# Two groups of loads put off, a row of norms written from another queue, and three additions moved in an attention and gated-FFN kernel

## The chip, the cores and the metric

The kernel runs on one core of a Trainium2 chip. The metric is the device time of one execution in microseconds (us); the number quoted is the median of several executions.

## The reference

Four batches, each with 6016 rows and 256 channels. Attention runs over channels, so its score matrix is 256 x 256 per batch; the result, 24064 rows of 256, goes through a gated feed-forward layer with 1536 hidden units.

```python
qn = q / (norm(q, axis=1) + 1e-6)          # q, k, v: (4, 6016, 256)
kn = k / (norm(k, axis=1) + 1e-6)
s = kn.transpose(0, 2, 1) @ qn / tau       # (4, 256, 256), tau = 1
a = exp(s - s.max(-1)); a /= a.sum(-1) + 1e-9
x = (v @ a).reshape(24064, 256)
out = (sigmoid(x @ w_gate) * (x @ w_val)) @ w_out
```

## The kernel before, in words

**Folding.** The softmax matrix of a batch is small, so the kernel multiplies it into the two weight matrices first: G = a @ w_gate and H = a @ w_val (tiles `gh_G`, `gh_H`, 16 pieces a batch in batch 0, 12 later). Then only v has to be streamed: gate = v @ G, val = v @ H, hidden = sigmoid(gate) * val, out = hidden @ w_out.

**Tiling.** A batch has 47 row tiles of 128 rows, in 12 chunks of four (three in the last). A chunk runs over 12 slots f, one per 128 hidden units. `glu(b, ci, f)` (L495) does a slot: two 512-column matmuls into `ps_gate`, two into `ps_val` (two PSUM banks each, so a slot's matmuls need the banks of two slots ago to be read out), a tanh on ACT into `g_sb` (L516), and on DVE `hT` = (g_sb + 1) * ps_val (L517). The output product of a chunk is done one chunk later, in pieces spread over the next chunk's slots (`run_work`), as a Strassen-like scheme with seven products; its sums of hidden tiles are made by DVE (`sums`, L539, in slots 7 to 11 of the chunk itself and 1 and 3 to 6 of the next). ACT copies a finished `ps_o` to `m_sb` (L593) or `out_sb` (L600), and POOL (GpSimd) makes the last additions (L594, L595, L610, L611). Batch 0's chunk 0 has a plain product and no sums.

**Order of the work.** It is written out by hand: instructions stay on each engine in the order in which the Python emits them. `side_work(b)` (L749) builds a table of side jobs for a batch; `at(slot, fn, ...)` puts one behind slot `slot` (chunk * 12 + f) of batch b. Such jobs are, for the batch after: loading q and k by groups of four tiles (`load_qk`, L138, issued by POOL, cast to bf16 on the way), the score matmuls (`score`, into `ps_s`), squares on ACT (`acc_square`, L248) and their running sums on DVE (`acc_add`, L286), and at the end the norms and the softmax. In batch 0 the groups start at slots s0 = 14, 20, 27, 34, 41, 48, 55, 61, 68, 75, 82, 89, and the additions stand at s0 + 3 and s0 + 7 (none for the first group). Loads of v (`load_v`, L148) are issued by POOL two chunks ahead, at f = 0; a chunk of v is transposed by a DMA from SP (`transpose_v`, L481) one chunk ahead, at f = 2. SP also issues the output stores (L652). All these queues work through their instructions in order, so an instruction that waits holds up those behind it.

**Start.** Batch 0 has no batch before it: its scores run alone, to about 33 us. Then come its softmax and the first four pieces of G and H. Pieces 4 to 15 are put between the slots of chunk 0: `gh_mid` (L813) names the piece that goes between the gate and the val matmuls of slot f, `gh_end` (L814) those behind it. POOL meanwhile loads v, the weights and w_out, in float32, casts w_out (`copy_w_out`, L212, slot 8) and makes sums of its blocks (`w_sums`, L217, from slot 10).

**Norms.** Behind slot 108 of a batch (chunk 9, f = 0) `norms_inv` (L361, L362) makes the inverse norms of the next batch, one value a channel. Those of k have to lie along a row on all partitions: `spread_both` (L313) transposes them on DVE into `rT` (L317), writes a row of 256 values to DRAM with two DMAs (L320) and reads it back to all 128 partitions (L324, `rk_sb`), all on SP's queue. `scale_x` (L304, `x_sb`) uses it on DVE behind slots 120 and 122.

Of the kernel before, what the change touches and what calls it, by code (L numbers as in the profile page):

```python
# [9 lines left out]
FP32 = mybir.dt.float32  # L10
# [43 lines left out]
def kernel(  # L54
# [20 lines left out]
    nc = tc.nc  # L75
# [5 lines left out]
    B, N, C = q.shape  # L81
# [4 lines left out]
    FC = DFF // P  # L86
# [15 lines left out]
    def pool(name, bufs, **kw):  # L102
        return ctx.enter_context(tc.tile_pool(name=name, bufs=bufs, **kw))
# [14 lines left out]
    dpool = pool("dpool", 1, space=bass.MemoryType.DRAM)  # L118
# [8 lines left out]
    def mm(out, lhsT, rhs, start, stop, **kw):  # L127
        nc.tensor.matmul(out, lhsT=lhsT, rhs=rhs, start=start, stop=stop, **kw)  # L128
# [23 lines left out]
    t0, nt = groups0[0]  # L152
# [72 lines left out]
    st = {}  # L225
# [87 lines left out]
    def spread_both(b):  # L313

        s = st[b]
        rT = attp.tile([P, 32], FP32, tag="rT", name="rT")
        nc.vector.transpose(out=rT, in_=r_wide)  # L317
        row = dpool.tile([C], FP32, tag="row", name="row")
        for i in range(CB):
            nc.sync.dma_start(  # L320
                out=row[ds(i * P, P)].rearrange("(s j) -> s j", j=32), in_=rT[CB + i : P : 32, :]
            )
        s["rk_sb"] = attp.tile([P, C], FP32, tag="rk", name="rk_sb")
        nc.sync.dma_start(out=s["rk_sb"], in_=row.rearrange("(o c) -> o c", o=1).to_broadcast([P, C]))  # L324

# [115 lines left out]
    gh_first = [(f0, nf, w, i) for f0, nf in pieces for w in range(2) for i in range(CB)]  # L441

    def gh_mms(b, piece, pl, tag):
        s = st[b]
        f0, nf, w, i = piece
        ps = pl.tile([P, FG], FP32, tag=tag, name="ps_gh")
        for j in range(CB):
            mm(
                ps[:, :nf],
                s["e"][i][:, j, :],  # L450
                w_sb[w][f0 // FG][:, j, ds(f0 % FG, nf)],
                start=(j == 0),
                stop=(j == CB - 1),
            )
        return ps

    def gh_store(b, piece, ps, act):
        s = st[b]
        f0, nf, w, i = piece
        dst = s["gh"][w][f0 // FG][:, i, ds(f0 % FG, nf)]  # L460
        if act:
            nc.scalar.activation(out=dst, in_=ps[:, :nf], func=ACT.Copy, scale=s["rrow"][i][w])
        else:
            nc.vector.tensor_scalar(  # L464
                out=dst, in0=ps[:, :nf], scalar1=s["rrow"][i][w], scalar2=None, op0=ALU.mult
            )

    def gh(b, piece, pl, tag, act=None):
        gh_store(b, piece, gh_mms(b, piece, pl, tag), piece[3] == 0 if act is None else act)
# [25 lines left out]
    def glu(b, ci, f, between=None):  # L495
        t0, nt = groups[ci]
        n = nt * P
        G, H = st[b]["gh"]
        vT = vts[b, ci]
        if f == 0:  # L500
            hts[b, ci] = hpool.tile([P, FC, CH], BF16, tag="hT", name="hT")
        ps_gate = psg.tile([P, CH], FP32, tag="g", name="ps_gate")
        ps_val = psv.tile([P, CH], FP32, tag="v", name="ps_val")
        for ps, w in ((ps_gate, G), (ps_val, H)):
            for ib in range(CB):
                mm(
                    ps[:, :n],
                    w[f // (FG // P)][:, ib, ds(f % (FG // P) * P, P)],
                    vT[:, ib, :nt, :],
                    start=(ib == 0),  # L510
                    stop=(ib == CB - 1),
                )
            if between is not None and w is G:
                between()
        g_sb = gpool.tile([P, CH], FP32, tag="g", name="g_sb")
        nc.scalar.activation(out=g_sb[:, :n], in_=ps_gate[:, :n], func=ACT.Tanh, scale=0.5)  # L516
        nc.vector.scalar_tensor_tensor(  # L517
            out=hts[b, ci][:, f, :n],
            in0=g_sb[:, :n],
            scalar=1.0,  # L520
            in1=ps_val[:, :n],
            op0=ALU.add,
            op1=ALU.mult,
        )
# [171 lines left out]
    for g, (t0, nt) in enumerate(groups0):  # L696
# [6 lines left out]
        while adds:  # L703
            w, last_sq = adds.pop()
# [44 lines left out]
    def side_work(b):  # L749


        side = {}

        def at(slot, fn, *a):
            side.setdefault(divmod(slot, FC), []).append((fn, a))

        for ci in range(NCH):
            nb, nci = (b, ci + 1) if ci + 1 < NCH else (b + 1, 0)
            lb, lci = (b, ci + 2) if ci + 2 < NCH else (b + 1, ci + 2 - NCH)
            if nb < B:  # L760
                at(ci * FC + 2, transpose_v, nb, nci)
            if lb < B:
                at(ci * FC + 0, load_v, lb, lci)
            if (b, ci) == (0, 0):
                for i in range(FC // TPC):
                    at(8, copy_w_out, i)
                for n, m in enumerate((1, 0, 3, 2, 4)):
                    for i in range(FC // TPC):
                        at(10 + 2 * n, sum_w_out, m, i)
        n = b + 1  # L770
        if n == B:
            return side
        first, last = (14 if b == 0 else 0), 8 * FC
        for g, (t0, nt) in enumerate(groups):
            s0 = first + g * (last - first) // NCH
            if b == 0:
                at(max(0, s0 - 12), load_qk, n, t0, nt)
            elif s0 >= 24:
                at(s0 - 24, load_qk, n, t0, nt)
            for u in range(nt):  # L780
                at(first + (t0 + u) * (last - first) // NT, score, n, t0, u)
            if g == 0:
                at(s0, acc_start, n)
            for i, (fn, w) in enumerate(((acc_square, 0), (acc_add, 0), (acc_square, 1), (acc_add, 1))):
                at(s0 + 1 + 2 * i, fn, n, g, w)
        if n + 1 < B:
            for g, (t0, nt) in enumerate(groups[:3]):
                at(NCH * FC - 24 + 8 * g, load_qk, n + 1, t0, nt)
        s0 = 8 * FC + 2
        at(s0 if b == 0 else s0 - 2, acc_fold, n, 0)  # L790
        at(s0 + 1 if b == 0 else s0, acc_fold, n, 1)
        at(s0 + 3, norms_mm, n)
        at(s0 + 4, root_seed, n)
        at(s0 + 4, root_steps, n)
        at(s0 + 10, norms_inv, n)
        at(s0 + 10, spread_both, n)
        at(s0 + 22, scale_x, n, 0)
        at(s0 + 24, scale_x, n, 1)
        at(s0 + 25, exps, n, 0)
        at(s0 + 26, exps, n, 1)  # L800
        at(s0 + 28, all_sums, n)
        at(s0 + 28, gh_tiles, n)
        for i, piece in enumerate(gh_order):
            slot = s0 + 29 + 2 * i
            if slot < NCH * FC:
                at(slot, gh, n, piece, *((pss, "s"), (psm, "m"))[i % 2])
            else:
                spill.setdefault((n, *divmod(slot - NCH * FC, FC)), []).append((gh, (n, piece, psm, "m")))
        return side

    gh_mid = {0: 4, 1: 6, 2: 9, 3: 11}  # L813
    gh_end = {0: (5,), 1: (7, 8), 2: (10,), 3: (12,), 4: (13,), 5: (14,), 6: (15,)}  # L814
    gh_banks = ((pso, "o"), (psm, "m"), (pso, "o"), (pss, "s"))

    def gh_piece(n):
        gh(0, gh_first[n], *gh_banks[n % 4])

    prev = None  # L820
    for b in range(B):
        side = side_work(b)
        for ci in range(NCH):
            final = (b, ci) == (B - 1, NCH - 1)
            for f in range(FC):
                mid = gh_mid.get(f) if (b, ci) == (0, 0) else None
                glu(b, ci, f, None if mid is None else (lambda: gh_piece(mid)))
                if prev is not None:
                    if f == 4:
                        store()  # L830
                    if f + final in NEXT_SLOTS and prev != (0, 0):
                        a_sum(*prev, 1, NEXT_SLOTS[f + final])
                    run_work(work, 1 / max(1, FC - final - f))
                if f in OWN_SLOTS and not final and (b, ci) != (0, 0):
                    a_sum(b, ci, 0, OWN_SLOTS[f])
                for fn, a in spill.get((b, ci, f), []) + side.get((ci, f), []):
                    fn(*a)
                if (b, ci) == (0, 0):
                    for i in gh_end.get(f, ()):
                        gh_piece(i)  # L840
            prev = (b, ci)
            if not final:
                work = out_work(*prev)
# [39 lines left out]
```

## Time and profile before

| | |
|---|---|
| median of 5 executions | 804.85 us (804.54 to 805.21) |
| the profiled execution | 804.54 us, span 802.8 us |
| granted TensorE clock, mean | 0.998 |
| busy: PE / DVE / ACT / POOL | 780.7 / 712.4 / 525.1 / 356.0 us |
| chain that ended last | PE 92%, DMA 6%, DVE 1%, POOL 1%, issue 1% |

PE is TensorE's matmuls, PEld its weight loads, DVE the vector engine, ACT the scalar engine, POOL GpSimd, SP the engine that issues most hardware DMAs. A row of the timeline reads: start, duration, engine, line, operation, tiles written and read, shapes, and how many instructions of the kind were merged; in brackets, the engine's idle time before it and what released it. A matmul's duration includes the fill of its pipeline, so the pitch of the work is read from start to start. In the waits a line reads: who waited, for whom, us in total, times, longest. In a DMA view q0 is the queue of POOL's transfers (software-made descriptors) and q1 that of SP's; both run on the same 16 DMA engines.

### The profile page before, as it was taken

The numbers are of one execution on the slowest core, as the hardware profiler recorded it, in microseconds if no ns is written. First come the engines' busy times: TensorE is split into PE (matmuls) and PEld (weight loads), VectorE is DVE, ScalarE is ACT, GpSimd is POOL, SyncE is SP. The second block draws the span as 40 slices with busy tenths as digits, with TensorE's granted clock in tenths as the row PEclk, the third lists the DMA queues.
The fourth block names the chain that finished last, engine by engine and source line by source line (L and its number), as shares of the span: only waits on it lengthen the run. The fifth ranks groups of instructions, "written<-read, shape, count | busy, mean of one in ns | idle before, by whom it ended". The sixth has DMA issues, their size and how long they took to land.

```text
span 802.8 us, 17831 instructions
## 1 busy us (share of the span) xinstructions
PE 780.7 (97%) x6719; PEld 497.8 (62%) x6733; DVE 712.4 (89%) x1216; ACT 525.1 (65%) x887; POOL 356.0 (44%) x568
## 2 busy tenths in 40 slices
PE   3899999999999999999999999999999999999998
PEld 2546666666666666666666666666666566666666
DVE  5767999999979999999987999999998898998995
ACT  3766777766667776775666767776666566666664
POOL 4573545435552454335443544443534244444433
PEclk9999999999999999999999999999999999999999
DMA  9995759523666458521576477524223323433402
GB/s 212 205 213 112 124 91 132 109 54 66 127 120 113 87 106 143 87 53 42 117 133 107 86 132 116 103 54 93 60 61 84 68 54 76 82 55 77 74 31 73
DMA packets 79399, 78.89 MB, mean 98 GB/s; under 512 B 51920, under 2 KB 57168, under 8 KB 79312
## 3 DMA queue, kind: packets, MB, share of 16 engines
q0 software_dynamic: 22192, 39.59, 30.5%
q1 hardware_dynamic: 56544, 37.30, 21.1%
q8 instruction: 52, 0.85, 0.5%
q10 hardware_dynamic: 576, 0.85, 0.3%
q14 instruction: 35, 0.29, 0.1%
HBM read 79.04 MB, written 24.64 MB: 129 GB/s over the span
## 4 chain that ended last, share of the span: by engine, by line
PE 92%; DMA 6%; DVE 1%; POOL 1%; issue 1%; POOLq 0%
PE ps_val L128 29%; PE ps_gate L128 29%; PE ps_o L128 27%; PE ps_s L128 4%; DMA k_sb<-in_k_dram 3%; PE ps_gh L128 2%; DMA vT<-v_sb 2%; DMA v_sb<-in_v_dram 1%; DVE hT L517 0%; DVE acc L286 0%; DVE sums L539 0%; POOL w_gate L197 0%; POOL w_val L197 0%; PE ps_end L128 0%; POOL q_sb L138 0%
## 5 line engine op out<-in xcount | busy, mean ns | idle before, releaser
L516 ACT ACTIVATE g_sb<-ps_gate 128x512 f32<-128x512 f32 (+1 forms) x576 | 338.5, 588 | 226.8 <-PE ps_gate L128 214.9
L517 DVE SCALAR_TENSOR_TENSOR hT<-g_sb,ps_val 128x512 bf16<-128x512 f32 (+1 forms) x576 | 384.9, 670 | 71.2 <-ACT g_sb L516 61.1
L128 PE MATMUL ps_gate<-vT,gh_G 128*128 128x512 bf16 (+1 forms) x1152 | 337.7, 375 | 1.0 <-DMA vT<-v_sb 1.0
L128 PE MATMUL ps_val<-vT,gh_H 128*128 128x512 bf16 (+1 forms) x1152 | 337.7, 375 | 0.3 <-DVE hT L517 0.3
L539 DVE TENSOR_TENSOR sums<-hT 128x768 bf16<-128x768 bf16 (+1 forms) x460 | 281.3, 612 | 0.0
L128 PEld LDWEIGHTS <-sums 128*128 128x128 bf16 x2670 | 183.0, 98 | 81.9 <-DVE sums L539 0.5
L128 PEld LDWEIGHTS <-gh_H 128*128 128x128 bf16 x1152 | 112.7, 98 | 131.6 <-DVE gh_H L464 0.8
L610 POOL TENSOR_TENSOR out_sb<-out_sb,m_sb 128x256 f32<-128x256 f32 x89 | 77.8, 874 | 233.7 <-ACT out_sb L600 202.6
L128 PE MATMUL ps_o<-w_sums,sums 128*128 128x128 bf16 x1602 | 154.2, 219 | 0.0
L128 PEld LDWEIGHTS <-hT 128*128 128x128 bf16 x1200 | 88.2, 98 | 46.9
L594 POOL TENSOR_TENSOR m_sb<-m_sb 128x128 f32<-128x128 f32 x89 | 42.5, 478 | 157.2 <-ACT m_sb L593 157.2
L128 PEld LDWEIGHTS <-gh_G 128*128 128x128 bf16 x1152 | 96.5, 98 | 16.0 <-DMA vT<-v_sb 1.5
L128 PE MATMUL ps_o<-w_out_sb,sums 128*128 128x128 bf16 x1068 | 96.2, 219 | 0.0
L128 PE MATMUL ps_o<-w_sums,hT 128*128 128x128 bf16 x1068 | 95.5, 219 | 0.0
L128 PE MATMUL ps_s<-k_sb,q_sb 128*128 128x256 bf16 x376 | 69.4, 287 | 15.7 <-DMA k_sb<-in_k_dram 8.7
L611 POOL TENSOR_TENSOR out_sb<-out_sb 128x256 f32<-128x256 f32 x89 | 77.2, 867 | 7.0
L600 ACT COPY out_sb<-ps_o 128x512 f32<-128x512 f32 x89 | 52.1, 586 | 12.3 <-PE ps_o L128 10.1
L286 DVE TENSOR_TENSOR acc<-acc,sq 128x1024 bf16<-128x1024 bf16 (+1 forms) x66 | 59.8, 906 | 0.0
L595 POOL TENSOR_TENSOR m_sb<-m_sb 128x128 f32<-128x128 f32 x89 | 53.4, 600 | 7.0
L248 ACT ACTIVATE sq<-k_sb 128x1024 bf16<-128x1024 bf16 (+2 forms) x44 | 44.8, 1027 | 12.0 <-DMA k_sb<-in_k_dram 12.0
L128 PEld LDWEIGHTS <-q_sb 128*128 128x128 bf16 x376 | 33.0, 103 | 20.8 <-issue 10.2
L593 ACT COPY m_sb<-ps_o 128x384 f32<-128x384 f32 x89 | 42.5, 478 | 3.7 <-PE ps_o L128 1.0
(85 smaller groups left out, 302.1 us busy)
## 6 DMA issues: line engine op xcount, KB each, us to landing
out_dram<-out_sb SPq DMA_DIRECT2D x43, 512.0 KB, 3.4
v_sb<-in_v_dram POOLq DMA_DIRECT2D x44, 256.0 KB, 5.2
q_sb<-in_q_dram POOLq DMA_DIRECT2D x35, 256.0 KB, 4.5
k_sb<-in_k_dram POOLq DMA_DIRECT2D x35, 256.0 KB, 5.6
q_sb<-in_q_dram POOLq DMA_DIRECT2D x4, 512.0 KB, 11.6
k_sb<-in_k_dram POOLq DMA_DIRECT2D x4, 512.0 KB, 13.5
w_f<-in_moe_w_out_dram POOLq DMA_DIRECT2D x3, 512.0 KB, 9.8
out_dram<-out_sb SPq DMA_DIRECT2D x3, 384.0 KB, 2.8
```

Source lines behind the costliest of these rows:

```text
L128: nc.tensor.matmul(out, lhsT=lhsT, rhs=rhs, start=start, stop=stop, **kw)
L248: nc.scalar.activation(out=sq[:, :nt, :], in_=src[:, :nt, :], func=ACT.Square)
L286: nc.vector.tensor_tensor(out=acc[:, :nt, :], in0=acc[:, :nt, :], in1=st[b]["sq", w][:, :nt, :], op=ALU.add)
L516: nc.scalar.activation(out=g_sb[:, :n], in_=ps_gate[:, :n], func=ACT.Tanh, scale=0.5)
L517: nc.vector.scalar_tensor_tensor(out=hts[b, ci][:, f, :n], in0=g_sb[:, :n], scalar=1.0, in1=ps_val[:, :n], op0=ALU.add, op1=ALU.mult,)
L539: nc.vector.tensor_tensor(out=sums[b, ci, g][:, m, :, : half * P], in0=hT[:, f0 + k0 : f1 : 2, ds(r0 * half * P, half * P)], in1=hT[:, f0 ...
L593: nc.scalar.copy(m, states[p]["ps"][:, : 3 * P].rearrange("p (n c) -> p n c", c=P))
L594: nc.gpsimd.tensor_tensor(out=m[:, 1, :], in0=m[:, 1, :], in1=m[:, 2, :], op=ALU.add)
L595: nc.gpsimd.tensor_tensor(out=m[:, 2, :], in0=m[:, 1, :], in1=m[:, 0, :], op=ALU.add)
L600: nc.scalar.copy(o[:, p : p + half + 1 : half, :], states[p]["ps"].rearrange("p (t c) -> p t c", c=C),)
L610: add(out=ends, in0=ends, in1=states[p]["m"][:, 1:3, :], op=ALU.add)
L611: add(out=ends, in0=ends, in1=mids, op=ALU.subtract)
```

## The change

Three loads of POOL move. v's third chunk of batch 0 (`load_v` for chunk 2, issued behind slot 0 of chunk 0) goes behind slot 9. So does the second q/k group of batch 1, which stood at slot 8. On POOL's queue the v load thereby moves behind the first q/k group and behind the three casts of w_out.

The row of norms is written from POOL's queue instead of SP's, and behind slot 109 instead of 108; the read (`read_row`, new) stays on SP, behind slot 111. On SP's queue the transpose of chunk 10 (slot 110) thereby stands ahead of the read. On POOL the two writes stand behind the load of v's chunk 11.

Additions of squares that fell on f = 8 go behind f = 10: in batch 0 those of slots 44, 68 and 92, and none in later batches.

The piece 7 of the first G and H goes from behind slot 1 to between slot 1's gate and val matmuls, behind piece 6. On DVE its store then stands ahead of slot 1's `hT`.

```diff
-        row = dpool.tile([C], FP32, tag="row", name="row")
+        row = s["row"] = dpool.tile([C], FP32, tag="row", name="row")
         for i in range(CB):
-            nc.sync.dma_start(
+            nc.gpsimd.dma_start(
                 out=row[ds(i * P, P)].rearrange("(s j) -> s j", j=32), in_=rT[CB + i : P : 32, :]
             )
+
+    def read_row(b):
+        s = st[b]
+        row = s["row"]
         s["rk_sb"] = attp.tile([P, C], FP32, tag="rk", name="rk_sb")
         nc.sync.dma_start(out=s["rk_sb"], in_=row.rearrange("(o c) -> o c", o=1).to_broadcast([P, C]))
...
-                at(ci * FC + 0, load_v, lb, lci)
+                at(ci * FC + (9 if (b, ci) == (0, 0) else 0), load_v, lb, lci)
...
-                at(max(0, s0 - 12), load_qk, n, t0, nt)
+                at(s0 - 12 if g == 0 else max(FC - 3, s0 - 12), load_qk, n, t0, nt)
...
-            for i, (fn, w) in enumerate(((acc_square, 0), (acc_add, 0), (acc_square, 1), (acc_add, 1))):
-                at(s0 + 1 + 2 * i, fn, n, g, w)
+            for w in range(2):
+                at(s0 + 1 + 4 * w, acc_square, n, g, w)
+                slot = s0 + 3 + 4 * w
+                at(slot + 2 if slot % FC == 8 else slot, acc_add, n, g, w)
...
-        at(s0 + 10, spread_both, n)
+        at(s0 + 11, spread_both, n)
+        at(s0 + 13, read_row, n)
...
-    gh_mid = {0: 4, 1: 6, 2: 9, 3: 11}
-    gh_end = {0: (5,), 1: (7, 8), 2: (10,), 3: (12,), 4: (13,), 5: (14,), 6: (15,)}
+    gh_mid = {0: (4,), 1: (6, 7), 2: (9,), 3: (11,)}
+    gh_end = {0: (5,), 1: (8,), 2: (10,), 3: (12,), 4: (13,), 5: (14,), 6: (15,)}
```

More of the change, by code (lines that the diff above doesn't have):

```diff
@@ L809, in side_work, with gh_pieces @@
         return side
-    gh_mid = {0: 4, 1: 6, 2: 9, 3: 11}
-    gh_end = {0: (5,), 1: (7, 8), 2: (10,), 3: (12,), 4: (13,), 5: (14,), 6: (15,)}
+    gh_mid = {0: (4,), 1: (6, 7), 2: (9,), 3: (11,)}
+    gh_end = {0: (5,), 1: (8,), 2: (10,), 3: (12,), 4: (13,), 5: (14,), 6: (15,)}
     gh_banks = ((pso, "o"), (psm, "m"), (pso, "o"), (pss, "s"))
-    def gh_piece(n):
-        gh(0, gh_first[n], *gh_banks[n % 4])
+    def gh_pieces(ns):
+        for n in ns:
+            gh(0, gh_first[n], *gh_banks[n % 4])
     prev = None
@@ L826 @@
                 mid = gh_mid.get(f) if (b, ci) == (0, 0) else None
-                glu(b, ci, f, None if mid is None else (lambda: gh_piece(mid)))
+                glu(b, ci, f, None if mid is None else (lambda: gh_pieces(mid)))
                 if prev is not None:
@@ L838 @@
                 if (b, ci) == (0, 0):
-                    for i in gh_end.get(f, ()):
-                        gh_piece(i)
+                    gh_pieces(gh_end.get(f, ()))
             prev = (b, ci)
```

## The prediction

> **What bounds the kernel now.** I read the page first: PE is busy 780.7 of 802.8 us, and the chain that ended last is 92% PE. So an edit can only pay where PE stands still, and I went to the waits (whole run, one line for each pair) and then to PE's timeline around each.
>
> ```profile
> PE ps_gate L128 <- DMA vT<-v_sb: 1.0, 1, 1.0
> PE ps_val L128 <- DVE hT L517: 0.3, 1, 0.3
> ```
>
> After batch 0's own scores and softmax these are the only PE lines: one wait for a transposed v chunk, one for DVE. The timeline gives place and true size:
>
> ```profile
> 50.97 0.59 PE L128 MATMUL ps_gate<-vT,gh_G 128*128 128x512 bf16 x2
> 51.40 0.59 PE L128 MATMUL ps_val<-vT,gh_H 128*128 128x512 bf16 x2
> 52.97 0.61 PE L128 MATMUL ps_gate<-vT,gh_G 128*128 128x512 bf16 x2 [0.97 <-DMA vT<-v_sb]
> ```
>
> A pair of 512-column matmuls starts 0.43 us after the pair before it (50.97 to 51.40; the 0.59 includes the pipeline's tail). The next was due at 51.83 and started at 52.97: **1.14 us** lost at chunk 1's first matmul. By the same pitch:
> - at 102.47 a val pair follows a gate pair of 101.57 by 0.90 instead of 0.43: **0.47**;
> - at 168.90 a val pair follows one of 168.35 by 0.55: **0.12**;
> - at 40.84 the val pair of batch 0's third slot holds the next matmul until 41.46, 0.62 instead of 0.43: **0.19** (its second half waits for the gh_H piece that DVE stores at 40.70).
>
> Together 1.92 us, or 0.24% of 804.54, the time of the profiled execution (span 802.8, 1.7 around it). The change does not touch the stalls of the first score phase or the tail. So 1.92 is the most it can give.
>
> **Part 1: v's third chunk and the second q/k group to slot 9.** POOL's queue before:
>
> ```profile
> 38.49 0.55 POOL L148 DMA_DIRECT2D v_sb<-in_v_dram  x1 [0.25 <-DMA w_gate<-in_moe_w_gate_dram]
> 40.04 0.55 POOL L138 DMA_DIRECT2D q_sb<-in_q_dram  x1 [0.99 <-DVE gh_G L464]
> 41.25 0.53 POOL L138 DMA_DIRECT2D k_sb<-in_k_dram  x1 [0.67 <-ACT gh_G L462]
> 48.16 1.04 POOL L212 CAST w_out_sb<-w_f 128x1024 bf16<-128x1024 f32 x1 [0.53 <-PE ps_gate L128]
> 49.15 0.53 POOL L138 DMA_DIRECT2D q_sb<-in_q_dram  x1
> ```
>
> The 38.49 load goes behind the 48.16 cast, in front of the 49.15 pair. SP transposes chunk 1 by DMA from 40.74, on queue q1, while POOL's loads fill q0 of the same engines. The DMA view, for 46 to 49.6 us and then for 50.75 to 51.5 (packets, MB, share):
>
> ```profile
> q0 software_dynamic: 358, 0.76, 96.6%
> q1 hardware_dynamic: 358, 0.09, 17.2%
> ```
> ```profile
> q0 software_dynamic: 43, 0.06, 85.1%
> q1 hardware_dynamic: 401, 0.10, 78.7%
> ```
>
> Packet for packet: while q0 has a backlog, the transpose gets as many packets as q0, 99 per us; as q0 runs dry it gets 535 per us (and 884 in the us from 62). It has 1056 packets in all, of which 78 are done by 46. A v load is 144 packets; without it the backlog ends 144/99 = 1.45 us sooner, near 49.3 instead of 50.75. By then 78 + 3.3 x 99 = 405 are done; the other 651 take 0.74 us (at 884) to 1.22 us (at 535), so to 50.0 to 50.5. PE started about 0.6 us after the last packet (52.4 to 52.97), which makes 50.6 to 51.1. PE wants it at 51.83 - 0.19 = 51.64. The late load stays clear of this: issued after the cast, at 49.20, it can show its first packet 1.27 to 2.67 us later (the spread of q0's first packets after POOL issues at 80.00 and at 89.00), at 50.5 to 51.9. Bounds: 0 (the tail packets crawl as they did from 51.5 to 52.4) to 1.14; I take **1.14**, since half a us of margin is left. What is late next: nothing near. v's third chunk is wanted by PE near 70, its transpose ran in 3.6 us when q0 was quiet; the second group's first score stands at slot 20 (the ps_s of 65.55), and loads of that stretch took 8.8 and 10.1 us to land, from 49.7 to 50.3 on: 60.4. The casts are where they were.
>
> **Part 2: piece 7 of the first gh before slot 1's val pair.** The same 0.43 us of matmuls, moved by one pair. The DVE store (0.48) then runs ahead of hT (0.69, after 40.09), which shifts by about 0.2, to end near 41; the val pair that reuses its bank stands at 42.75. **0.19**; bounds 0 to 0.19.
>
> **Part 3: additions off slot 8 (three of them, batch 0 only).** DVE, then POOL, at the 0.47 us stall:
>
> ```profile
> 99.64 1.04 DVE L539 TENSOR_TENSOR sums<-hT 128x768 bf16<-128x768 bf16 x1
> 100.61 1.21 DVE L286 TENSOR_TENSOR acc<-acc,sq 128x1024 bf16<-128x1024 bf16 x1
> 101.74 0.68 DVE L517 SCALAR_TENSOR_TENSOR hT<-g_sb,ps_val 128x512 bf16<-128x512 f32 x1
> ```
> ```profile
> 99.55 0.72 POOL L610 TENSOR_TENSOR out_sb<-out_sb,m_sb 128x256 f32<-128x256 f32 x1 [2.05 <-ACT out_sb L600]
> 100.35 0.93 POOL L611 TENSOR_TENSOR out_sb<-out_sb 128x256 f32<-128x256 f32 x1
> ```
>
> Sums that take 0.55 alone and acc that takes 0.68 alone (the groups' short cases) become 1.04 and 1.21 when a POOL addition runs: they take turns, and the one already waiting goes first. With acc two slots on, hT starts near 100.7 instead of 101.74 and ends at 101.3, before PE's 102.0. So 0.47 and 0.12 go (**0.59**; bounds 0 to 0.59).
>
> But the second addition moves from slot 68 to 70, and the next group's stands at 71, its sums with it. I replay chunk 5's end from DVE's and POOL's rows. Before:
>
> ```profile
> 137.20 0.54 DVE L539 TENSOR_TENSOR sums<-hT 128x768 bf16<-128x768 bf16 x1
> 137.67 1.21 DVE L286 TENSOR_TENSOR acc<-acc,sq 128x1024 bf16<-128x1024 bf16 x1
> 138.81 1.27 DVE L517 SCALAR_TENSOR_TENSOR hT<-g_sb,ps_val 128x512 bf16<-128x512 f32 x2
> ```
> ```profile
> 137.32 1.01 POOL L610 TENSOR_TENSOR out_sb<-out_sb,m_sb 128x256 f32<-128x256 f32 x1 [1.13 <-ACT out_sb L600]
> 138.41 1.06 POOL L611 TENSOR_TENSOR out_sb<-out_sb 128x256 f32<-128x256 f32 x1
> ```
>
> The hT of 138.81 ends near 139.45, and PE's val pair at 139.82 needs it (two banks): 0.37 us of slack. After: slot 10's hT ends at 135.8 (g_sb ready 135.17), its sums at 136.3, the moved acc at 136.9 (0.60 from start to start), slot 11's hT at 137.5. The POOL addition of 137.32 is now ahead of slot 11's sums: sums to 138.45, POOL's second to 139.1, acc to 139.65, hT to 140.3, 0.5 past 139.82. A **new wait of 0.5**; bounds 0 (if sums get in ahead of POOL by a margin of 0.15, hT ends at 139.85) to 0.7. I take 0.5, the replay's own value. The third moves to 94 and meets shorter operations (0.55) and no sums at slot 96; its val pairs keep over 0.6.
>
> **Part 4: the row of norms from POOL, the read two slots on.** Three times; nothing of it is on the chain now. The transpose behind it on SP is freed sooner, where no PE wait stood: 0. Its cover, batch 1:
>
> ```profile
> 187.65 1.18 SPq L320 DMA_DIRECT2D row<-rT  x2
> 189.91 0.33 SPq L324 DMA_DIRECT2D rk_sb<-row  x1
> ```
>
> x_sb, its reader, starts at 201.84, and the read lands in 3.5: 8.4 us of slack. After: rT is ready near 189.2 (behind sums of 188.11), two POOL issues (0.55 each) end near 190.3, first packet 1.27 to 2.67 later, then 1.0 to 2.6 until SP reads (the waits at L324), then 3.8: 196.4 to 199.4. In batch 2 POOL's v load, ahead of the row, was issued only at 382.96: the row lands 391 to 393.8 against x_sb at 394.51. Behind the waiting POOL issue stand m_sb additions (POOL idles 56%), behind SP's read one output store and one transpose, wanted 20 us later. Cost: 0, up to some us if it came late.
>
> The Trainium skill, "SBUF — State Buffer", section "Reading the diagram", speaks against this part: a DMA issued from GpSimd has its descriptors written there, and DVE's two-port operations lock that out; it gives 0.62 us alone and 3.1 beside such an operation. By it, an estimate, each row would come 2.5 us later, batch 2's up to 1.8 us past x_sb, and the sum below would fall to about nothing. No row here shows such a delay on its own; the spread of 1.27 to 2.67 may hold some of it.
>
> **Sum.** 1.14 + 0.19 + 0.59 - 0.50 = 1.42 us: 804.54 to 803.1 in its profile, and from the median of 804.85 to **803.4**. A measurement here can tell about 0.2% (1.6 us) from no change, and the forecast lies just inside.
>
> **The rivals.**
> - *No new wait at slots 70 and 71* (0.30): gain 1.92, 802.9 to 803.0. For: the replay turns on 0.15 us, and accs at slot 10 (58, 82) cost nothing before. Against: those had no acc at 11 behind them.
> - *The transposed chunk still comes late* (0.17), so the change misses its main aim: the freed queue is filled too soon, or the slow packets of 51.5 to 52.4 have another cause. 0.6 to 1.1 comes back: 804.0 to 804.5.
> - *Slower: the row comes late* (0.06). Place: DVE's queue at x_sb, in batches 1 to 3, where hT stands behind it. It decides from 2.4 us past my latest landing in batch 1 and from 0.7 in batch 2; 2 us beyond in all three costs 6, less 1.4: 809.4. Over 0.2% slower needs 3.0 us of lateness in sum.
>
> The forecast has 0.47. Some of its spread (a new wait of 0.3) falls under 803.24, and most of the first rival: faster by over 0.2% 0.34, within 0.60, slower 0.06. The range 802.6 to 804.8 takes in the bounds of all but the last.
>
> **What would show it.** In the changed profile: no PE wait for vT near 52, its transpose landing before 51.6; no gap at 41; no wait for hT near 101 and 167; a wait of about 0.5 at chunk 6's third val pair, near 138.5; x_sb with no idle time before it. A vT wait that stays, or idle DVE before x_sb, would make the prediction wrong.

## The result, and the profile after

| | before | after |
|---|---|---|
| median | 804.91 us (48 executions) | 803.07 us (28 executions, 802.80 to 803.84) |
| ratio of the medians | | 0.9979 [0.9973, 0.9984] |
| profiled execution, span | 804.54, 802.8 | 803.04, 801.3 |
| first gate matmul | 36.81 | 36.78 |
| from there to the last matmul | 762.21 | 760.88 |
| from there to the end of the span | 3.74 | 3.60 |

The change takes 1.84 us off the median, 0.16% to 0.27%. (One execution of before took 4704 us and one of p1_loads 1674 us; they move their medians by at most 0.02 us.) The two profiled executions differ by 1.50: before's lay 0.37 below its own median, after's 0.03. Of the 1.50, 1.33 lies between the first gate matmul and the last matmul, where the change works; 0.17 is start and tail.

The page of after, its span, its busy times and its chain:

```profile
span 801.3 us, 17849 instructions
...
PE 780.7 (97%) x6719; PEld 497.7 (62%) x6733; DVE 711.6 (89%) x1216; ACT 525.0 (66%) x887; POOL 358.9 (45%) x574
...
PE 94%; DMA 3%; DVE 1%; issue 1%; POOL 0%; ACT 0%; POOLq 0%; DVEq 0%
```

PE is busy for the same 780.7 us; the span is shorter only by what PE stood still. The chain says the same: DMA's share falls from 6% to 3%, as the chain no longer goes through the transposed chunk. After 36 us, PE's waits are one line:

```profile
PE ps_val L128 <- DVE hT L521: 0.3, 1, 0.3
```

(Lines of the code past L328 are four higher in after: `hT` is L521, `sums` L543.) The vT line is gone. The hT line looks like the one of before and is not: it stands in another place, as PE's timeline of after shows, first at chunk 1, then at chunk 6:

```profile
51.19 0.59 PE L128 MATMUL ps_val<-vT,gh_H 128*128 128x512 bf16 x2
51.77 0.61 PE L128 MATMUL ps_gate<-vT,gh_G 128*128 128x512 bf16 x2
...
137.73 0.59 PE L128 MATMUL ps_gate<-vT,gh_G 128*128 128x512 bf16 x2
138.58 0.59 PE L128 MATMUL ps_val<-vT,gh_H 128*128 128x512 bf16 x2 [0.25 <-DVE hT L521]
```

Read from start to start, with 0.43 us as the pitch of a pair: the gate pair was due at 51.62 and came at 51.77, so 0.15 us of the old 1.14 is left, too short for the list of waits. The val pair of 138.58 was due at 138.16: a new stall of 0.42, where the list says 0.25, since an idle time is counted from the modelled end of the matmul before. The stalls near 41, 101.3 and 167 are gone. So, gap by gap: 0.98 + 0.18 + 0.47 + 0.12 - 0.42 = 1.33 us, the whole of what lies between first gate and last matmul.

**Why the transposed chunk came earlier.** The DMA queues of after, first for 46 to 49.6 us, then for 49.6 to 50.75 and for 50.75 to 51.5 (packets, MB, share):

```profile
q0 software_dynamic: 331, 0.66, 87.0%
q1 hardware_dynamic: 554, 0.14, 24.5%
```
```profile
q1 hardware_dynamic: 382, 0.10, 129.6%
q0 software_dynamic: 16, 0.03, 16.7%
```
```profile
q0 software_dynamic: 27, 0.06, 78.5%
q8 instruction: 1, 0.02, 10.4%
q1 hardware_dynamic: 63, 0.01, 8.4%
```

In the first window before had 358 packets on each queue; now q0 runs dry inside it, and the transpose (q1) moves 554. Nearly alone, it moves 382 in 1.15 us, but not evenly: 307 from 49.5 to 50.0, then 61 in the next half us. The last 63 come slowly too, the last near 51.2. In that last window v's load is already there: issued at 49.30, as POOL's timeline shows, behind the third cast, it brings its first packet at 50.56.

```profile
48.32 1.04 POOL L212 CAST w_out_sb<-w_f 128x1024 bf16<-128x1024 f32 x1 [0.55 <-DMA w_f<-in_moe_w_out_dram]
49.30 0.53 POOL L148 DMA_DIRECT2D v_sb<-in_v_dram  x1
49.82 0.54 POOL L138 DMA_DIRECT2D q_sb<-in_q_dram  x1
```

**Why the new stall came.** DVE's timeline of after, at chunk 5's end:

```profile
134.61 0.68 DVE L286 TENSOR_TENSOR acc<-acc,sq 128x1024 bf16<-128x1024 bf16 x1
135.22 0.68 DVE L521 SCALAR_TENSOR_TENSOR hT<-g_sb,ps_val 128x512 bf16<-128x512 f32 x1
135.81 0.98 DVE L543 TENSOR_TENSOR sums<-hT 128x768 bf16<-128x768 bf16 x1
136.72 1.21 DVE L286 TENSOR_TENSOR acc<-acc,sq 128x1024 bf16<-128x1024 bf16 x1
137.85 1.27 DVE L521 SCALAR_TENSOR_TENSOR hT<-g_sb,ps_val 128x512 bf16<-128x512 f32 x2
```

and POOL's beside it:

```profile
135.66 0.72 POOL L614 TENSOR_TENSOR out_sb<-out_sb,m_sb 128x256 f32<-128x256 f32 x1 [1.47 <-ACT out_sb L604]
136.45 0.93 POOL L615 TENSOR_TENSOR out_sb<-out_sb 128x256 f32<-128x256 f32 x1
```

POOL's first addition (135.66) starts just ahead of the sums (135.81), which take 0.98 instead of 0.55; its second, waiting by then, goes ahead of the second acc (136.72), which takes 1.21 instead of 0.68. The hT that PE needs starts at 137.85.

**The row of norms.** Batch 1 in after: POOL writes the row, SP reads it, DVE uses it, with no idle time in brackets before x_sb:

```profile
188.03 1.15 POOL L320 DMA_DIRECT2D row<-rT  x2 [0.27 <-DVE rT L317]
```
```profile
191.15 0.33 SPq L328 DMA_DIRECT2D rk_sb<-row  x1
```
```profile
200.48 0.48 DVE L304 SCALAR_TENSOR_TENSOR x_sb<-ps_s,r_wide,rk_sb 128x256 f32<-128x256 f32 x1
```

The read lands 3.0 us after its issue, near 194.1: 6.3 us ahead of x_sb; in batches 2 and 3 it is 4.4 and 6.5.

### The profile page after: what moved, and what is told of

Same layout as the page of the kernel before. It is cut to its first block, busy times and chain, and to the rows that moved or that the text cites. A ratio compares the mean times of both kernels' runs of the same rounds, so it can differ in the third digit from the quotient of the medians.

```text
span 801.3 us, 17849 instructions
## 1 busy us (share of the span) xinstructions
PE 780.7 (97%) x6719; PEld 497.7 (62%) x6733; DVE 711.6 (89%) x1216; ACT 525.0 (66%) x887; POOL 358.9 (45%) x574
## 4 chain that ended last, share of the span: by engine, by line
PE 94%; DMA 3%; DVE 1%; issue 1%; POOL 0%; ACT 0%; POOLq 0%; DVEq 0%
PE ps_gate L128 30%; PE ps_val L128 30%; PE ps_o L128 27%; PE ps_s L128 4%; DMA k_sb<-in_k_dram 3%; PE ps_gh L128 2%; DVE hT L521 0%; POOL q_sb L138 0%; PE ps_end L128 0%; DVE acc L286 0%; POOL k_sb L138 0%; ACT sq L248 0%; PE ps_n L128 0%; DVE x_sb L382 0%; PE ps_r L128 0%
## 5 line engine op out<-in xcount | busy, mean ns | idle before, releaser
L521 DVE SCALAR_TENSOR_TENSOR hT<-g_sb,ps_val 128x512 bf16<-128x512 f32 (+1 forms) x576 | 384.8, 670 | 70.8 <-ACT g_sb L520 60.4
L543 DVE TENSOR_TENSOR sums<-hT 128x768 bf16<-128x768 bf16 (+1 forms) x460 | 281.8, 613 | 0.0
```

The costliest lines, as they stand in the source:

```text
L521: nc.vector.scalar_tensor_tensor(out=hts[b, ci][:, f, :n], in0=g_sb[:, :n], scalar=1.0, in1=ps_val[:, :n], op0=ALU.add, op1=ALU.mult,)
L543: nc.vector.tensor_tensor(out=sums[b, ci, g][:, m, :, : half * P], in0=hT[:, f0 + k0 : f1 : 2, ds(r0 * half * P, half * P)], in1=hT[:, f0 ...
```

## The experiments

Each kernel is after (or before) with one edit. "Gap" is time lost by PE from start to start, in the profiled execution. The kernels ran in three series, each beside executions of before (medians 804.78, 804.92 and 804.73), so medians of different series are to be compared through their ratios to before.

| kernel | median | ratio [95%] | gap at vT, 51.8 | new gap, 138.6 |
|---|---|---|---|---|
| p1_loads | 803.49 | 0.9984 [0.9975, 0.9993] | 0 | 0 |
| v_back | 804.47 | 0.9995 [0.9986, 1.0003] | 1.31 | 0.42 |
| v_mid | 804.38 | 0.9994 [0.9985, 1.0003] | 1.22 | 0.42 |
| p3_adds | 804.58 | 0.9998 [0.9989, 1.0007] | 1.07 | 0.42 |
| keep68 | 802.53 | 0.9972 [0.9961, 0.9982] | 0.24 | 0 |
| acc72 | 802.56 | 0.9973 [0.9963, 0.9984] | 0.09 | 0 |
| norms_sp | 803.31 | 0.9982 [0.9973, 0.9991] | 0.46 | 0.42 |
| late_row | 803.10 | 0.9979 [0.9970, 0.9987] | 0.34 | 0.42 |
| after_again | 803.05 | 0.9981 [0.9972, 0.9990] | 0 | 0.42 |
| best | 802.46 | 0.9972 [0.9961, 0.9984] | 0 | 0 |
| best_norms_sp | 802.87 | 0.9978 [0.9969, 0.9987] | 0.05 | 0 |

**p1_loads: the loads alone.** Before, with only the two lines of the loads changed.

```diff
-                at(ci * FC + 0, load_v, lb, lci)
+                at(ci * FC + (9 if (b, ci) == (0, 0) else 0), load_v, lb, lci)
...
-                at(max(0, s0 - 12), load_qk, n, t0, nt)
+                at(s0 - 12 if g == 0 else max(FC - 3, s0 - 12), load_qk, n, t0, nt)
```

> The kernel before with part 1 alone: v's third chunk and the second q/k group behind slot 9. Theory (gaps add up): the wait for the transposed v chunk near 52 falls from 1.14 us to 0 to 0.2, the gaps near 41 (0.19), 102 (0.47) and 169 (0.12) stay, so 1.0 us less than before, 803.9 from 804.9. Rival (the gain belongs to the norms' row or to the parts together): less than 0.5 us, 804.4 or more.

The vT gap went, the other three stalls of before stayed (0.18, 0.47, 0.11). The time fell by 1.29 us, with an interval of 0.6 to 2.0. So the loads are the larger part of the change.

**v_back: after without the v load's move.**

```diff
-                at(ci * FC + (9 if (b, ci) == (0, 0) else 0), load_v, lb, lci)
+                at(ci * FC + 0, load_v, lb, lci)
```

> The changed kernel with v's third chunk issued behind slot 0 again; the second q/k group stays behind slot 9. Theory (the v load's 144 packets lengthen the backlog that halves the transpose's share of the DMA engines): the wait near 52 comes back in full, and by 0.19 more, since PE arrives earlier: about 1.1 to 1.3 us at that place, 1.0 to 1.2 us slower than the change, 804.1 to 804.3. Rival (the q/k group's place is what counts): no difference, 803.1.

PE's timeline of v_back shows the old wait again, and the time cannot be told from before:

```profile
51.18 0.59 PE L128 MATMUL ps_val<-vT,gh_H 128*128 128x512 bf16 x2
52.92 0.61 PE L128 MATMUL ps_gate<-vT,gh_G 128*128 128x512 bf16 x2 [1.15 <-DMA vT<-v_sb]
```

With p1_loads it encloses the part: with v's load behind the casts the gap is 0 to 0.46, with it behind slot 0 it is 1.1 to 1.3, whatever else is changed. The other half of part 1, the q/k group, stays moved in v_back and takes nothing off this gap.

**v_mid: is it the backlog, or the place in the program?** v's load behind slot 7, where POOL issues it ahead of the casts.

```diff
-                at(ci * FC + (9 if (b, ci) == (0, 0) else 0), load_v, lb, lci)
+                at(ci * FC + (7 if (b, ci) == (0, 0) else 0), load_v, lb, lci)
```

> The changed kernel with v's third chunk behind slot 7: behind the first q/k group on POOL's queue, but ahead of the three casts, so issued near 41 instead of 49.3. Theory (what counts is the backlog on q0 while the transpose runs, whatever stands first in it): the wait near 52 is back as with the load at slot 0, about 1.3 us, 804.3 to 804.5. Rival (what counts is that the q/k group goes ahead of the v load): no wait, 803.1.

POOL's timeline of v_mid: the load goes out at 40.86, 2.4 us later than in before but ahead of the casts:

```profile
39.88 0.55 POOL L138 DMA_DIRECT2D k_sb<-in_k_dram  x1 [0.71 <-ACT gh_H L466]
40.86 0.53 POOL L148 DMA_DIRECT2D v_sb<-in_v_dram  x1 [0.44 <-DMA v_sb<-in_v_dram]
```

The vT gap is there in full (1.22), and the gain is gone. Seven slots in the program are worth nothing while the load stays in the backlog that the transpose shares; what counts is that its packets come after the transpose's.

**p3_adds: the additions alone.** Before, with the lines of `acc_add` of the change.

> The kernel before with part 3 alone: the three additions two slots later. Theory: the waits near 102 (0.47) and 169 (0.12) go, one of 0.42 near 139.8 comes, 0.17 us faster than before, 804.7, which the times alone cannot tell from no change. Rival (the wait at chunk 6 needs the other parts): 0.6 us faster, 804.3.

The gaps at 101 and 167 went, 0.42 came at 139.66, and the vT gap stayed. The time fell by 0.15 us, which cannot be told from nothing. By itself this part returns nearly all that it takes: 0.59 - 0.42.

**keep68: the addition of slot 68 left where it was,** so that no two additions follow each other.

```diff
-                at(slot + 2 if slot % FC == 8 else slot, acc_add, n, g, w)
+                at(slot + 2 if slot in (44, 92) else slot, acc_add, n, g, w)
```

> The changed kernel with the addition of slot 68 left at 68; those of 44 and 92 stay moved. Theory (additions at slots 70 and 71 behind one another make DVE late): the wait of 0.42 us at 138.6 goes and none comes in its place, 0.4 us faster than the change, 802.65. Rival (slot 8 is bad in all three places): a wait of 0.1 to 0.5 appears near chunk 5's last slots and the time stays at 803.1.

The stall went and nothing took its place. PE's timeline of keep68:

```profile
137.74 0.59 PE L128 MATMUL ps_gate<-vT,gh_G 128*128 128x512 bf16 x2
138.17 0.59 PE L128 MATMUL ps_val<-vT,gh_H 128*128 128x512 bf16 x2
138.60 0.39 PE L128 MATMUL ps_o<-w_sums,hT 128*128 128x128 bf16 x4
```

0.43 us from gate to val. The median is 0.5 below after's and the profiled span 0.4; the intervals of the two ratios overlap, so it is the profile that shows the gain. So moving slot 68's addition took away nothing and made the new stall.

**acc72: slot 70, or two in a row?** The addition of 68 stays moved to 70, that of 71 goes to 72. (In batches 1 and 2 an addition at slot 71 moves too; PE has no stall there in after or in acc72.)

```diff
-                at(slot + 2 if slot % FC == 8 else slot, acc_add, n, g, w)
+                at(slot + 2 if slot % FC == 8 else slot + (slot == 71), acc_add, n, g, w)
```

> The changed kernel with the addition of slot 71 one slot later, at 72; the one of 68 stays moved to 70. Theory (additions behind two slots in a row that both have sums leave DVE late): the addition at 72 stands in a slot without sums, the wait of 0.42 us near 138.6 goes or falls under 0.15, 0.3 to 0.4 us faster than the change. Rival (the addition at slot 70 by itself is what costs): the wait stays at 0.42 and so does the time.

DVE's timeline of acc72:

```profile
135.59 0.97 DVE L543 TENSOR_TENSOR sums<-hT 128x768 bf16<-128x768 bf16 x1
136.49 0.67 DVE L521 SCALAR_TENSOR_TENSOR hT<-g_sb,ps_val 128x512 bf16<-128x512 f32 x1
137.09 0.68 DVE L286 TENSOR_TENSOR acc<-acc,sq 128x1024 bf16<-128x1024 bf16 x1
```

The sums are stretched by POOL as in after (0.97), but hT comes next, at 136.49 instead of 137.85, and the acc behind it costs nothing. An addition at slot 70 does no harm; a second one behind it, before the next hT, does.

**norms_sp: the row back on SP's queue.**

```diff
-            nc.gpsimd.dma_start(
+            nc.sync.dma_start(
...
-        at(s0 + 11, spread_both, n)
-        at(s0 + 13, read_row, n)
+        at(s0 + 10, spread_both, n)
+        at(s0 + 10, read_row, n)
```

> The changed kernel with part 4 undone: the row of norms written and read by SP, behind slot 108. Theory (that part is hidden on both sides): no difference within 0.2 us of the change, 803.1, and no new PE wait. Rival (part of the measured gain, which is 0.4 to 0.5 us more than the PE waits that the two profiles show, belongs to it): 0.3 to 0.5 us slower, 803.4 to 803.6.

No PE wait near the norms appears, in either place of the row. The median is 0.24 us above after's, just past the 0.2 that I had allowed, but this profile also has a longer vT gap (0.46 against 0.15), which is the whole of the 0.3 between the two profiled spans (801.6 and 801.3). So the difference is no reading of the row.

**late_row: the row later, to price the slower rival.** The write goes behind slot 115, the read behind slot 117.

```diff
-        at(s0 + 11, spread_both, n)
-        at(s0 + 13, read_row, n)
+        at(s0 + 17, spread_both, n)
+        at(s0 + 19, read_row, n)
```

> The changed kernel with the row of norms written six slots later (behind slot 115) and read behind slot 117. By the changed kernel's profile the read lands 6.3, 4.3 and 6.5 us ahead of x_sb in batches 1, 2 and 3; six slots are 7.5 us. Theory (the prediction's slower rival has its place and price right): DVE waits at x_sb for 1.2, 1.5 (its write starts from rT, not from the v load, so 1 to 3) and 1.0 us, PE for about 0.4 less each, 1.5 to 3.5 us slower than the change, 804.6 to 806.6. Rival (a late row is covered by other work on DVE): under 0.5 us, 803.1 to 803.6.

The median did not move, so the size I expected was wrong: x_sb waited for 0, 0.34 and 1.71 us in batches 1 to 3, where I had 1.2, 1.5 and 1.0. DVE's timeline of late_row at the x_sb of batches 2 and 3, then PE's at the latter:

```profile
393.72 0.48 DVE L304 SCALAR_TENSOR_TENSOR x_sb<-ps_s,r_wide,rk_sb 128x256 f32<-128x256 f32 x1 [0.34 <-DMA rk_sb<-row]
...
587.76 0.48 DVE L304 SCALAR_TENSOR_TENSOR x_sb<-ps_s,r_wide,rk_sb 128x256 f32<-128x256 f32 x1 [1.71 <-DMA rk_sb<-row]
588.16 0.68 DVE L521 SCALAR_TENSOR_TENSOR hT<-g_sb,ps_val 128x512 bf16<-128x512 f32 x1
```
```profile
587.81 0.59 PE L128 MATMUL ps_gate<-vT,gh_G 128*128 128x512 bf16 x2
588.89 0.59 PE L128 MATMUL ps_val<-vT,gh_H 128*128 128x512 bf16 x2 [0.49 <-DVE hT L521]
```

0.34 us of idle DVE cost PE nothing; 1.71 cost 0.65 (1.08 from start to start, less 0.43). So DVE runs about 1 us ahead of PE there, and a late row is paid only past that. The row was also less late than I had set out: from POOL's issue to SP's read took 2.3 us in batches 1 and 2, against 3.1 and 3.4 in after.

Batch 3's 1.71 need not stand in other executions: the profiled one, at 803.90, is the slowest of its eleven. There the second of POOL's two writes landed 3.50 us after its issue, where the other five of the kernel took 1.6 to 1.7. Its last two packets start only at 583.62, as a fetch of instructions that began at 582.71 ends. The DMA queues for 582.6 to 583.7 show these three packets and nothing else. That the fetch held the two up is a reading, not tested.

```profile
q8 instruction: 1, 0.02, 5.3%
q0 software_dynamic: 2, 0.00, 0.3%
```

**best: keep68, with the loads still later.** v's chunk and the q/k group behind slot 11, so that v is issued at 51.20.

```diff
-                at(ci * FC + (9 if (b, ci) == (0, 0) else 0), load_v, lb, lci)
+                at(ci * FC + (11 if (b, ci) == (0, 0) else 0), load_v, lb, lci)
...
-                at(s0 - 12 if g == 0 else max(FC - 3, s0 - 12), load_qk, n, t0, nt)
+                at(s0 - 12 if g == 0 else max(FC - 1, s0 - 12), load_qk, n, t0, nt)
...
-                at(slot + 2 if slot % FC == 8 else slot, acc_add, n, g, w)
+                at(slot + 2 if slot in (44, 92) else slot, acc_add, n, g, w)
```

> The changed kernel with the addition of slot 68 left there, and with v's third chunk and the second q/k group behind slot 11, so behind POOL's first three sums of w_out, some 2 us later. Theory (what is left of the wait near 52, 0.15 us in the changed kernel and 0.24 with slot 68 kept, is the late load's first packets meeting the transpose's last): the wait goes, 0.1 to 0.3 us faster than with slot 68 kept, 802.3 to 802.5. Rival (the tail of the transpose has another cause): 802.5 to 802.7, the wait as it was.

PE's timeline of best, then its DMA queues for 50.75 to 51.5:

```profile
51.13 0.59 PE L128 MATMUL ps_val<-vT,gh_H 128*128 128x512 bf16 x2
51.57 0.60 PE L128 MATMUL ps_gate<-vT,gh_G 128*128 128x512 bf16 x2
```
```profile
q1 hardware_dynamic: 18, 0.00, 2.4%
```

The gate pair follows at the plain pitch, and its profile has no PE wait after 37 us. The transpose ends near 51.0 here too, with no packet of q0 in the window: so v's first packets are not what slows its tail. The wait went, but not by the theory: the third cast, and the chunk with it, came 0.2 us earlier than in keep68 (the table in the next section). In time best cannot be told from keep68 (802.46 in six executions and 802.53 in eight); by their medians both lie 0.5 to 0.6 us below after and 2.2 to 2.5 below before of their series, and their intervals overlap after's.

**best_norms_sp: best with norms_sp's edit,** to read the row of norms with next to no vT gap.

> The fastest version so far (slot 68 kept, late loads behind slot 11) with the row of norms written and read by SP behind slot 108 again. It has no wait for the transposed chunk that could vary between runs. Theory (part 4 is hidden): 802.4 to 802.6, as with POOL's row, and no PE wait in its profile. Rival (part 4 gives some of the gain): 802.8 or more.

The profiled span is 800.6, as in best, and the profile shows no PE wait. The median is 0.4 above best's, on the rival's side of what I expected. But the two are from different series, best has only six executions, the ratios' intervals overlap over most of their length, and the profiled execution (802.41) is the fastest of its eleven, so that no profile shows what the slower ones spend. Whether part 4 is worth anything up to 0.4 us stays open.

**before_again and after_again: the spread.** No edit, one more profile of each.

> The kernel before, unchanged, for a second profile: the medians differ by 1.84 us, the two profiles' spans by 1.5. Theory (the wait for the transposed chunk differs from run to run in the kernel before): the time lies within 804.3 to 805.4, the wait near 52 is other than 1.14 by about as much as the time is other than 804.54, and the waits near 41, 102 and 169 are the same within 0.02. Rival (the variation lies in the first score phase or the tail): the wait is 1.14 again.

> The changed kernel, unchanged, beside these others on one chip, with a second profile. Theory: 803.0 to 803.2; the wait near 138.6 is 0.42 again, set by instruction order alone; the wait for the transposed chunk near 52, which was 0.15 to 0.46 in four kernels that share that stage, is again somewhere from 0 to 0.5, and with it the time. Rival: both are as before within 0.02.

before_again's profiled execution took 804.17, 0.37 less than the first one of before, with the same gaps within 0.03 (1.16 at vT). What differed was outside the change: the first gate matmul stood 0.28 earlier and the tail was 0.13 shorter. So for this pair of executions the theory fell and the rival held. after_again had no vT gap at all, and the new gap again at 0.42.

## Why the prediction was right, step by step

- **What bounds it.** Right. Only the gaps of PE paid: 1.33 us of gaps, in a stretch that is 1.33 us shorter.
- **Part 1, mechanism.** Right: v_back and v_mid bring the wait back when the load stands in the backlog again. The end of the backlog near 49.3 held too: the transpose moved 38 packets from 48.5 to 49.0 and 196 from 49.0 to 49.5.
- **Part 1, size.** The term of 1.14 was a little large: 0.98 in after's profile. The step that failed is the rate at which I let the last packets go. By 49.3 there were 423 packets done, near my 405. The other 633 took until 51.2, at some 330 per us in place of the 535 to 884 that I had used, so they were done 0.7 to 1.2 us later than my 50.0 to 50.5 and the half a us of margin was used up. The sign that I had named, a landing before 51.6, was missed: the chunk landed at 51.73. The bound I named for it (the tail crawls as before) is what half happened. What is left of the gap differs among kernels with the same stage, and it goes with the time of the third cast of w_out. That cast waits for the last load of w_out, behind which only the first q/k group is left in the backlog:

| | third cast starts | gate pair starts | gap |
|---|---|---|---|
| best_norms_sp | 48.01 | 51.52 | 0.05 |
| after_again | 48.06 | 51.60 | 0 |
| acc72 | 48.13 | 51.55 | 0.09 |
| best | 48.14 | 51.57 | 0 |
| p1_loads | 48.29 | 51.76 | 0 |
| after | 48.32 | 51.77 | 0.15 |
| keep68 | 48.37 | 51.78 | 0.24 |
| norms_sp | 48.46 | 51.88 | 0.46 |
| late_row | 48.46 | 51.92 | 0.34 |

In the five kernels with a gap of 0.09 or more PE started 3.41 to 3.46 us behind that cast. The transposed chunk landed 3.36 to 3.42 us behind it in the six of these profiles that show the landing, best among them (51.51, when PE was due at 51.56). So the chunk comes at a nearly fixed time after that cast, and PE waits if it is ready sooner; that best and after_again show no gap at all is the luck of the profiled execution. In best v is issued two us later, and its chunk comes no sooner behind the cast: the load put off is not in the way where the change has it. What makes the last packets slow is not settled (in best two fetches of instructions run beside them, and the last packet of a load starts at 50.48); no run took the fetches away.
- **Part 2.** 0.19 forecast, 0.18 found. It was seen only within the whole change, not alone.
- **Part 3, gain.** 0.59 forecast, 0.59 found, in after and in p3_adds.
- **Part 3, the new wait.** 0.50 forecast, 0.42 found, at 138.58 where I had placed it at 138.5, and by the replayed order: POOL's addition first, by 0.15 us, then sums, then acc. POOL's addition starts 0.15 or 0.16 us ahead of the sums in after, after_again, norms_sp, late_row, v_back, v_mid and p3_adds alike. The first rival fell; keep68 and acc72 show the cause to be the two additions in a row.
- **Part 4.** No cost, as forecast, but on a row that came earlier than I had let it: landing near 194.1 and 388.7, against 196.4 to 199.4 and 391 to 393.8. My estimate of 2.5 us more for each row, from the Trainium skill's two figures ("SBUF — State Buffer", section "A bandwidth-pool intuition that's wrong (but worth ruling out)"), finds no support here. The page's 3.1 us is for a DMA beside a DVE `tensor_copy`; beside these writes DVE ran `hT` and `sums`, which are other operations, so the estimate was wrongly drawn. In after the six writes landed 2.2 to 3.1 us after POOL's issue, with the packets of the v load that POOL had issued before still ahead of them, and x_sb never waited. In late_row no load stood ahead, and five of six landed in 1.6 to 1.7.
- **The slower rival** did not happen, and its price was wrong: I let all of a row's lateness reach PE, and late_row shows, in the one wait long enough to tell, that the first us or so of it is hidden by DVE's lead; by its batch 3 (1.71 for 0.65), 2 us in each of three batches would cost about 2.8 us, an estimate, and not 6.
- **The sum.** 1.42 forecast from the profile, 1.50 found between the profiles, of which 0.17 is start and tail that I had not counted, against 0.09 too much in the gaps. The rest of the 1.84 between medians is the profiled execution of before, which lay 0.37 below its median. The forecast of 803.4 is 0.3 above the 803.07 found.

## What to carry to other kernels

When PE waits for a DMA on one queue, count what shares its engines on the others: a load that nobody needs for 20 us can hold back one that is needed now, and it must be moved behind the needed transfer's packets, not only behind some instructions. When work is moved out of a crowded slot, replay the engines' order at the place where it lands; one of the three additions moved here had caused no stall and made a new one. A late operand costs what is left after its reader's lead over the bound engine, so measure that lead before pricing the lateness.

## What the runs showed of the hardware

Two queues with work shared the DMA engines packet for packet (358 to 358 in 3.6 us in before), although the transpose's packets are small (0.09 MB against 0.76 MB): a transpose beside large loads was paced here by the number of the loads' packets, not by their bytes, and went from 99 packets per us to 332 (382 in 1.15 us) when nearly alone.

The end of such a transfer is uneven: in after, single packets around 50.6 to 51.1 us, most of them v's, took 0.5 to 0.8 us each, and a 16 KB fetch of instructions 1.25 us. The whole stage also shifts from run to run: the third cast started anywhere from 48.01 to 48.46 in kernels that do the same up to there.

While POOL's additions run, DVE behaves as if the two took turns: sums went from 0.55 to between 0.97 and 1.04 us and acc from 0.68 to 1.21, and at the same place that was the same in each profile to within 0.1 us. An order decided by 0.15 us came out the same in all seven profiles named above, and cost 0.42 each time; acc72 has the same order too, and there, with no second addition before the next hT, it cost nothing.
